# The five engines' hand-written orders replaced by another set, with some seventy small operations on other engines

## Chip, core and metric

One core of a Trainium2 chip runs the whole program. The metric is the device time of one execution in microseconds (us), and the lower the better. The engines' names are those of the profile: PE multiplies matrices (PEld is its weight load), DVE is the vector engine, ACT the engine for exponentials and scaled copies, POOL a slower vector engine, SP the engine whose queue issues nearly all transfers (DMAs).

## What is computed

Attention that is masked by clusters feeds a two-layer block with a softmax gate and a layer norm. Cut to what matters:

```python
# q, k, v: 4 batches x 8 heads x 768 positions x 64; centroids: 8 heads x 16 x 64
q_assign = argmax(q_n @ c_n.T)            # the nearest of 16 centroids, for each position
k_assign = argmax(k_n @ c_n.T)
scores = where(q_assign == k_assign, q @ k.T / 8, -1e9)
attn = softmax(scores) @ v
x = attn, heads side by side              # 3072 tokens x 512
h = x @ w_in                              # 3072 x 1024
solu = h * softmax(h)
ln = (solu - mean) / sqrt(var + 1e-6) * g_ln
out = ln @ w_out                          # 3072 x 512
```

## The kernel before, in words

**Tiles and stages.** There are 16 pairs of heads (4 batches, 4 pairs each). For each pair, q and k are loaded and turned so that the head dimension lies on partitions (by PE for the first batch, operations `tp`, L396 and L403; by DVE for the others, `xt`, L444), PE scores them against the centroids (`cl`, L484 and L489), DVE finds the best centroid of each position (`tb`, `mx`, `oh`, `ot`), and 32 rows with the one-hot assignment are placed below the cast q and k (`ca`, L468 to L472; `pl`, L533 to L540; `bl`, L549), so that one matmul gives score and mask together.

The scores are worked off in 94 units of a few (head, 128-query block) pieces. A unit's scores lie in banks of PSUM, each 128 keys by 512 queries (by 384 in the first four units). `S24.0` is the scores of bank 0 of unit 24: PE writes them (function `scores`, L627; two matmuls of 256 columns, or one of 384 in the first four units). `E24.0` is the exponential of that bank on ACT (function `expo`, L635), and `V24.0` and `V24.1` are the products with v on PE (function `values`, L654, six matmuls of 65 columns each). `N` is the division on DVE (L666, L679). There are 294 banks. After a token tile of 128 has all its heads, `tx` turns x, `h` (96 operations of two matmuls of 512 columns, L744) and `y` (96 such, L813) are the two layers, and `hm`, `ex`, `u`, `tu`, `bn`, `ag`, `at`, `al`, `sc`, `ou` are the maximum, the exponential, the product, its turning, the norm's statistics, the scale and the store.

**What sets the order.** Every operation is entered with `add`: a name, an engine, a cost, what it needs, and a function that issues its instructions. The class `Weave` holds a text for each engine with the kinds in the order in which that engine runs them (`S2` means two operations of kind S, the next two that are not yet taken); within one engine nothing overtakes. The tables `AWAY` put single operations on another engine than their default. `run` walks through the five queues with the costs, gives each operation a start, and then issues all operations in the order of these starts, so the instruction order of each engine is the text's. The costs and the constants (`HOP`, `LANES`, `ring_s = 3`, `ring_e = 9`) are used for that walk alone; on the chip the instructions wait on semaphores that the tile framework sets from the tiles that they touch.

**Banks for scores.** The pool `ps_s` (L214) has three buffers of one bank, all with the tag `sps`. Score banks take them in turn (L622). Of the 25th to 66th bank, two in every five go to the region `hreg` instead (L614 to L616). A further tile of the same tag is made ahead of everything else: `idle_p` (L854). It takes the output of the filler matmuls: `idle(n)` (L856 to L859) issues n matmuls of 128 columns on a zeroed tile, with no reader. The operation `wm` is 25 of them at the start; each `fl` in PE's text is two more, and the text says where (L902 to L904). A tile of a pool holds its buffer until the last instruction in the program that touches it; the framework lets the next tile of that tag have the buffer from then on. In the kernel before, PE's text has `fl9`, the last filler, two operations ahead of `S0.0`.

**The start.** The first pair comes in halves. `tp0.0.x.y` turns half y of q (x = 0) or k (x = 1) of the first pair; `tp0.1.0.0` to `tp0.3.1.1` are the other pairs of batch 0, twelve operations of three matmuls. Their data come by two transfers of 384 KB for each pair (`load_twelve`, L377).

**The end.** The last tile but one (f = 22) and the last (f = 23) are turned by PE (`ptu`), copied to SBUF by `tu` (L738 on DVE, L740 on ACT), multiplied (`y`) and scaled by `sc` (L830 on ACT, L832 on DVE).

Of the kernel before, what the change touches and what calls it, by code (L numbers as in the profile page):

```python
# [22 lines left out]
class Weave:  # L23
# [18 lines left out]
    ORDER["PE"] = """
        fl wm tp2 cp fl4 cl tp2 fl4 cl fl tp S2 cq S tp S tp S2 tp S tp2 S2 cl S V3 S2 tp3 S gt V3
        S2 tp2 S tp S2 cl S3 V3 S7 V3 S3 cl S3 V4 S5 V2 S V2 S4 V S2 V3 S cl S3 V2 S V S2 V S me S3
        V S V3 me S3 ptx V2 S2 cl V S V S5 V2 h4 S2 h V2 S3 h V2 S V2 S h S2 h S V S V2 S V S h S2 h
        V S2 V2 S y3 V S2 y S h2 S2 V2 h2 S2 cl S V S V2 S V S h S2 h S V S V S h y4 S3 V3 h2 S2 V2
        S h S2 V y S y3 S2 V2 S cl S V S V S V2 S2 y S y S2 V3 S2 y S V S y S2 V2 S h S2 V3 S2 cl S
        V3 S3 cl S2 V2 S V2 S h2 S3 h V S V S V2 y3 S2 y V S2 V h S2 V S h S V S h2 S3 h V2 S2 V4 h
        S3 y3 S2 V y S2 V3 S2 h2 S3 V2 cl S3 V2 h S2 h cl V2 S2 V2 S h S2 h2 S2 V3 y S y S y S y V S
        V2 S h2 S2 h2 S3 V3 S V y3 V y V S2 h S cl S3 V2 h S2 h V S2 V S cl V2 S3 y2 S V S V y2 h2  # L50
        S2 V2 S h2 S3 cl S V3 S V S2 y3 S2 V y V S h S2 h V2 S h2 S3 h V2 S y2 S V2 S2 V2 y2 S2 h3
        S3 V2 h2 V y S3 y3 V3 S3 h2 S2 cl S V S V S V2 S y2 h V S2 h V S2 h2 S2 V S V h V4 S2 y2 h
        S3 V2 h2 S2 V2 S y2 S2 h2 y2 S h2 S2 V2 y S V2 S y h2 S3 h2 S2 V4 y S3 h2 y V S2 h2 V S V S
# [5 lines left out]
        bn hm tb N mx oh bn ag ot u xt2 hm cv N bn u bn2 tb mx hm bn N oh ag2 u ot xt2 hm bn N sc u
        bn tb ag cv N xt mx oh xt ot sc N bl xt2 tb bn N mx ca tb N mx oh ot hm oh N ot u xt bn3 ag  # L60
        xt N ag hm sc N ca u bn2 xt bl sc hm ag N xt tb mx u tb oh ot N hm mx xt oh u bn2 ot N hm bn
        ag xt ca u N bn tb xt2 mx ag hm tb N bn2 oh ot u xt2 N hm tb mx oh N ag bn bl u mx bn ot N
        bn oh hm ot ag xt u N bn xt ag hm bn2 ag u sc N bl hm ca tb mx cv2 oh u ot N bn2 hm N bl u
# [8 lines left out]
    """
    AWAY = {}
    AWAY.update(dict.fromkeys("""
        ca0.0.0.0.0 ca0.0.0.1.0 ca0.0.0.1.1 ca0.2.0.0 ca0.2.1.0 ca3.2.0.1 sc23.0 xa0.0.0.1 xa0.0.1.0
        xa0.1.1.1 xa0.2.0.0 xa0.2.0.1 xa0.2.1.0 xa0.2.1.1 xa0.3.0.0 xa0.3.1.0 xb0.0.1.1
    """.split(), "ACT"))
    AWAY.update(dict.fromkeys("""
        bl0.0.1 bl1.3 bl2.1 bl3.0 bl3.1 bl3.3 ca0.1.0.0 ca0.1.0.1 ca0.2.1.1 ca2.1.0.0 ca2.2.1.0
        ca3.0.0.1 ca3.3.1.0 cv0.0.0 cv0.1.0 cv1.1.0 cv1.2.0 cv3.1.1 cv3.2.1 cv3.3.0 pl0.0.0.0.1  # L80
        pl0.0.0.1.1 sc11 sc13 sc14 sc18 sc2 sc23.1 sc3 sc4 sc5 tu22.0
    """.split(), "DVE"))
    AWAY.update(dict.fromkeys("""
        ca0.0.1.1.1 pl0.0.0.0.0 pl0.0.0.1.0 pl0.0.1.0.0 pl0.0.1.1.0 pl1.0.0.0 pl1.0.0.1 pl1.0.1.0
        pl1.0.1.1 pl1.1.0.0 pl1.1.0.1 pl1.1.1.0 pl1.1.1.1 pl1.2.0.0 pl1.2.0.1 pl1.2.1.0 pl1.2.1.1
        pl1.3.0.0 pl1.3.0.1 pl1.3.1.0 pl1.3.1.1 pl2.0.0.0 pl2.0.0.1 pl2.0.1.0 pl2.0.1.1 pl2.1.0.0
        pl2.1.0.1 pl2.1.1.0 pl2.2.0.0 pl2.2.0.1 pl2.2.1.0 pl2.2.1.1 pl2.3.0.0 pl2.3.0.1 pl2.3.1.0
        pl2.3.1.1 pl3.0.0.0 pl3.0.0.1 pl3.0.1.0 pl3.1.0.0 pl3.1.0.1 pl3.1.1.0 pl3.1.1.1 pl3.2.0.0
        pl3.2.0.1 pl3.2.1.0 pl3.2.1.1 pl3.3.0.0
    """.split(), "POOL"))  # L90
    HOP = 0.17
    LANES = 8
# [1232 lines left out]
```

## Time and profile before

| what | value |
|---|---|
| time, median of 3 runs (lowest to highest) | 224.29 us (224.18 to 224.49) |
| span of the profiled execution | 222.4 us |
| granted PE clock in the profiled execution | 0.999 |
| DVE busy | 199.1 us (90%) |
| POOL busy | 126.6 us (57%) |
| DMA mean | 174 GB/s |

The profiled execution is one run of the same program, from its first to its last instruction; the median lies 1.9 us above its span, which is what lies around the span. An engine's busy time is the union of its instructions. Matmuls overlap in the records (the end of one is modelled), so PE's pace is read from the distance between starts, or from the chain of waits, where each piece stands with the time until the next. 30 matmuls of L744 and L813 have no record; those of L627 are complete, so a score bank is found by counting its matmuls.

### The profile page before, as it was taken

What the parts mean: (1) busy time and instruction counts of PE and PEld (TensorE: products, weight loads), DVE (VectorE), ACT (ScalarE), POOL (GpSimd) and SP (SyncE); (2) the same over time, 40 slices, a digit from 0 to 9 for tenths busy, and PEclk for the clock granted to TensorE, in tenths of its full rate; (3) what the DMA queues carried; (4) which work ended last, traced back from release to release, by engine and by line L of the source; (5) the groups of instructions that cost most, each with busy time, mean ns of one, the idle gap of its engine ahead of it and who ended that gap; (6) DMA issues with size and microseconds to landing.
All of it is one profiled execution on the core that took longest, in us unless ns stands there. A gap on an engine that the chain in (4) does not pass through costs nothing.

```text
span 222.4 us, 6852 instructions
## 1 busy us (share of the span) xinstructions
PE 214.8 (97%) x2518; PEld 151.8 (68%) x2548; DVE 199.1 (90%) x363; ACT 194.7 (88%) x382; POOL 126.6 (57%) x252
## 2 busy tenths in 40 slices
PE   8999899999999999999999999999999999999993
PEld 7765577767777687777777666676767767665452
DVE  2789999999999999899989999999999979999891
ACT  3899999999999999999999989999999989795352
POOL 3189597759884986188837674783746101226131
PEclk9999999999999999999999999999999999999999
DMA  6998989797799979899999897998922928565623
GB/s 157 352 388 221 193 165 284 203 172 165 127 175 237 180 141 215 136 193 166 153 211 239 156 185 150 151 168 158 230 99 50 115 78 145 117 165 121 166 98 143
DMA packets 122433, 38.74 MB, mean 174 GB/s; under 512 B 111448, under 2 KB 117152, under 8 KB 122400
## 3 DMA queue, kind: packets, MB, share of 16 engines
q1 hardware_dynamic: 121680, 37.82, 79.8%
q10 hardware_dynamic: 720, 0.49, 0.7%
q8 instruction: 20, 0.33, 0.7%
q14 instruction: 13, 0.11, 0.1%
HBM read 23.11 MB, written 6.29 MB: 132 GB/s over the span
## 4 chain that ended last, share of the span: by engine, by line
PE 91%; DVE 3%; issue 2%; ACT 2%; DVEq 0%; ACTq 0%
PE sps L627 27%; PE hreg L744 18%; PE yps L813 17%; PE ops L654 16%; PE csc L489 4%; PE hreg L627 2%; PE idle_p L859 2%; PE csc L484 1%; PE hreg L403 1%; PE hreg L396 1%; ACT qk L468 1%; PE hreg L813 1%; ACT e L635 1%; DVE u L763 1%; DVE w_sum L598 1%
## 5 line engine op out<-in xcount | busy, mean ns | idle before, releaser
L635 ACT ACTIVATE e<-sps 128x512 bf16<-128x512 f32 (+1 forms) x276 | 143.2, 609 | 10.2 <-PE sps L627 9.8
L627 PE MATMUL sps<-qk 96*128 96x256 bf16 (+5 forms) x600 | 87.4, 263 | 0.7 <-ACT e L635 0.4
L627 PEld LDWEIGHTS <-qk 96*128 96x128 bf16 (+1 forms) x636 | 59.6, 121 | 24.5 <-issue 8.8
L654 PEld LDWEIGHTS <-e 128*128 128x128 bf16 x1152 | 49.9, 97 | 9.3 <-issue 1.9
L654 PE MATMUL ops<-v,e 128*128 128x65 bf16 x1152 | 54.3, 193 | 0.4 <-DVE x L679 0.4
L744 PE MATMUL hreg<-w_in_sb,xT 128*128 128x512 bf16 x177 | 48.3, 378 | 0.8
L813 PE MATMUL yps<-w_out_c,uT 128*128 128x512 bf16 x169 | 45.1, 379 | 0.8
L540 POOL COPY qk<-oht 32x384 f32<-32x384 f32 (+1 forms) x49 | 24.2, 494 | 21.5 <-DVE oht L521 15.7
L763 DVE TENSOR_TENSOR u<-e_sb,hreg 128x1024 bf16<-128x1024 bf16 (+1 forms) x25 | 29.1, 1169 | 2.7 <-ACT e_sb L756 2.1
L774 DVE BATCH_NORM_STATS2 bs<-u 128x6 f32<-128x512 bf16 x48 | 31.3, 677 | 0.0
L750 DVE TENSOR_REDUCE nmax<-hreg 128x1 f32<-128x1024 f32 x24 | 29.1, 1213 | 2.0 <-PE hreg L744 1.7
L756 ACT ACTIVATE e_sb<-hreg,nmax 128x1024 bf16<-128x1024 f32 x24 | 26.9, 1121 | 4.5 <-DVE nmax L750 4.4
L790 POOL TENSOR_SCALAR esq<-es,mv 128x1 f32<-128x1 f32 x24 | 8.3, 344 | 33.6 <-DVE mv L778 30.3
L813 PEld LDWEIGHTS <-uT 128*128 128x128 bf16 x200 | 18.0, 97 | 13.1 <-issue 0.3
L744 PEld LDWEIGHTS <-xT 128*128 128x128 bf16 x192 | 17.6, 97 | 11.3 <-ACT e L635 0.3
L472 POOL TENSOR_SCALAR qk<-xt 64x768 bf16<-64x768 f32 (+1 forms) x27 | 22.2, 823 | 3.5 <-DVE xt L444 1.7
L444 DVE STREAM_TRANSPOSE xt<-raw 128x768 f32<-128x768 f32 x24 | 22.2, 949 | 0.0
L470 POOL CAST qk<-xt 64x768 bf16<-64x768 f32 (+1 forms) x25 | 20.9, 836 | 1.2
L679 DVE TENSOR_TENSOR x<-ops,den 128x256 bf16<-128x256 f32 (+1 forms) x39 | 18.9, 486 | 1.3
L784 POOL TENSOR_SCALAR es<-esum 128x1 f32<-128x1 f32 x24 | 5.6, 236 | 20.9 <-ACT e_sb L756 20.4
L793 POOL TENSOR_TENSOR alpha<-esq,halves 128x1 f32<-128x1 f32 x24 | 13.8, 574 | 2.0
L830 ACT ACTIVATE y<-yps,alpha 128x512 f32<-128x512 f32 x15 | 10.4, 695 | 4.3 <-PE yps L813 3.0
(85 smaller groups left out, 206.9 us busy)
## 6 DMA issues: line engine op xcount, KB each, us to landing
vf<-in_v_dram SPq DMA_DIRECT2D x16, 384.0 KB, 4.6
out_dram<-y SPq DMA_DIRECT2D x23, 256.0 KB, 2.5
raw<-in_q_dram SPq DMA_DIRECT2D x50, 96.0 KB, 3.8
raw<-in_k_dram SPq DMA_DIRECT2D x50, 96.0 KB, 3.0
w_g<-in_moe_w_out_dram SPq DMA_DIRECT2D x4, 512.0 KB, 8.3
w_st<-in_moe_w_in_dram SPq DMA_DIRECT2D x4, 512.0 KB, 6.2
raw<-in_q_dram SPq DMA_DIRECT2D x3, 384.0 KB, 6.0
raw<-in_k_dram SPq DMA_DIRECT2D x3, 384.0 KB, 7.8
```

The lines of the kernel that those rows point to most:

```text
L444: nc.vector.transpose(xt[:], raws[b, p, i][:].rearrange("p j c -> p (j c)"))
L472: VEC[e].tensor_scalar(dst, src, scalar1=inv_C, scalar2=1.0, op0=Alu.mult, op1=Alu.mult)
L540: ins = VEC[e].tensor_copy(dst.bitcast(F32), src.bitcast(F32).unsqueeze(1) .to_broadcast([NB, 2, n // 2]))
L627: ins = nc.tensor.matmul(sps_[n, k][:, c0:c0 + w], side(b, h // 2, 1, h % 2, keys)[r], side(b, h // 2, 0, h % 2, slice(s0 * P, s0 * P + w) ...
L635: ins = nc.scalar.activation(es[n, k][:, :w], sps_[n, k][:, :w], Act.Exp, scale=exp_scale, bias=-exp_scale)
L654: nc.tensor.matmul(opss[g][:, s, :VW], es[n, k][:, c0:c0 + P], v1[slot(b, h // 2)][:, h % 2, kt, :VW], start=(kt == 0), stop=(kt == n_t - 1))
L744: uses(nc.tensor.matmul(hreg[:, at(f, f2)[1], :], xTs[f][:, dc, :], w_in_sb[:, dc, f2 * FF2:(f2 + 1) * FF2], start=(dc == 0), stop=(dc == ...
L750: uses(nc.vector.tensor_reduce(ff[f, "nmax"][:], pair_of(f), axis=AXY, op=Alu.max, negate=True), *both(f))
L756: uses(nc.scalar.activation(ff[f, "e"][:], pair_of(f), Act.Exp, bias=ff[f, "nmax"][:], accum_out=ff[f, "esum"][:]), *both(f))
L763: uses(nc.vector.tensor_tensor(ff[f, "u"][:, r], ff[f, "e"][:, r], pair_of(f)[:, r], op=Alu.mult), *both(f)[r])
L774: nc.vector.bn_stats(ff[f, "bs"][:, f2, :], ff[f, "u"][:, f2, :])
L813: ins = nc.tensor.matmul(dst, ff[f, "uT"][:, at(f, f2)[0] * (n_fc // 2) + c, :], w_out_c[:, fc, cols], start=(fc == fcs[0] and turn == 0 i ...
```

## The change

Only the texts and the tables at the head of `Weave` differ: the order of all five engines, and the engine of 74 operations. No operation is added or taken away: PE has 733 before and after, with ten `fl` in both. Between engines there move: 12 of the `pl` from POOL to SP and 3 from SP to POOL, 3 from POOL to DVE, 1 from DVE to POOL; casts `ca`: 7 from DVE to POOL, 4 from POOL to DVE, 4 from POOL to ACT, 4 from ACT to POOL, 2 from ACT to DVE; `cv`: 6 from DVE to POOL, 5 back; `bl`: 5 from DVE to POOL, 3 back; copies `xa`: 3 from DVE to ACT, 3 from ACT to DVE; scales `sc`: 3 from DVE to ACT, 4 from ACT to DVE; both copies `tu22` from DVE to ACT.

The diff, cut:

```diff
     ORDER["SP"] = """
-        ld4 si ld3 lv lg ld3 lo lv lo ld2 lo2 lv ld6 lv ld8 li4 tx ld3 lv ld tx lv tu ld10 tx tu ld4
...
+        ld4 si ld4 lg lv ld lo lv ld5 lo ld5 lv ld2 lo ld lo ld lv ld li ld2 li3 ld3 tx ld2 tx lv ld
+        lv ld tu ld2 tx ld3 pl2 tu ld lv ld5 tu ld7 pl ou tu ld lv ld4 ou ld4 pl ld2 tu ld lv ld4 ou
...
     ORDER["PE"] = """
-        fl wm tp2 cp fl4 cl tp2 fl4 cl fl tp S2 cq S tp S tp S2 tp S tp2 S2 cl S V3 S2 tp3 S gt V3
-        S2 tp2 S tp S2 cl S3 V3 S7 V3 S3 cl S3 V4 S5 V2 S V2 S4 V S2 V3 S cl S3 V2 S V S2 V S me S3
-        V S V3 me S3 ptx V2 S2 cl V S V S5 V2 h4 S2 h V2 S3 h V2 S V2 S h S2 h S V S V2 S V S h S2 h
-        V S2 V2 S y3 V S2 y S h2 S2 V2 h2 S2 cl S V S V2 S V S h S2 h S V S V S h y4 S3 V3 h2 S2 V2
...
-        V y4 S2 V h4 S3 y V3 y S2 y2 h4 y S V3 y V y2 h ptx h y h2 y3 h2 y4 h2 ptu2 y8 ptu y4 ptu y4
+        fl wm fl tp2 cp tp cl tp3 cl tp2 S2 cq S tp S2 tp S tp S2 cl S3 tp V3 S tp gt S tp S V3 S cl
+        S3 tp S tp S V S V2 S fl S2 fl S4 V S V2 S2 cl S V S2 V S V2 S3 fl S3 V2 S V2 S fl S cl S V
+        S V3 S4 V S2 V2 S V S3 fl me S2 V4 me S3 V S2 ptx V S V S V S2 cl S V S V2 h S V S h S2 V S
+        h S h V S V S V S2 h S fl V h fl V2 S2 V h S2 h S2 h S V S V2 S2 V h S V y2 V S y2 S h2 S2 h
+        cl S h V2 S V S V S2 V2 h S2 h S h S V y V S V2 S y2 V y h S V S2 y S y S2 h S2 y2 V h V2 S2
+        V S cl S V S V S2 y S y V2 S2 V2 y S h V S V S y S2 h S2 h S V3 S cl S2 V h S2 V2 S2 cl S V
+        S V2 S V fl S2 y S V S y V S V2 y S3 V y h2 S2 V S V2 h S2 h S2 V h S2 h V2 S2 V2 S y3 V S y
...
+        S2 h3 S V2 y V2 y3 h ptx h y h2 y3 h2 y4 h2 ptu2 y8 ptu y3 ptu y5
     """
     ORDER["DVE"] = """
...
-        ag bn N ag2 u tx bn hm sc u bn2 hm tu2 bn ag2 u2 bn2 ag tu sc
...
+        u bn ag bn hm bn ag bn u ag N bn hm N u tx bn hm sc ag u bn2 hm bn2 ag2 u2 bn sc bn tu ag
+        sc3
     """
     ORDER["ACT"] = """
-        wa xa2 ca2 xa2 xb ca4 E6 xa E2 xa E xa ca E3 xa3 E4 ca E2 xa E53 ex E13 ex E5 sc E3 ex E11
...
-        tu sc2 oz
+        wa xa3 ca xa xb xa ca xa2 E8 xa E xa2 E3 ca E xa E64 ex E11 ex E5 sc E2 ex E8 ca E3 ex sc E8
+        sc ca E8 ex E25 ex E12 ex E5 sc E4 ex E13 ex E6 sc E3 ex E8 ca E10 ex E7 sc E6 ex E6 sc E4
...
+        sc ex sc tu3 oz
     """
```

Written out, the first part of PE's order is: before, `fl0 wm tp0.0.0.0 tp0.0.1.0 cp fl1 fl2 fl3 fl4 cl0.0.0 tp0.0.0.1 tp0.0.1.1 fl5 fl6 fl7 fl8 cl0.0.1 fl9 tp0.1.0.0 S0.0`; after, `fl0 wm fl1 tp0.0.0.0 tp0.0.1.0 cp tp0.0.0.1 cl0.0.0 tp0.0.1.1 tp0.1.0.0 tp0.1.0.1 cl0.0.1 tp0.1.1.0 tp0.1.1.1 S0.0`. The eight other fillers stand, after the change, behind `S3.3`, `S3.5`, `S8.1`, `S10.0`, `S14.1`, `S22.1`, `h1.0.1` and, as the last one, `fl9`, behind `S43.0 V41.1`.

More of the change, by code (lines that the diff above doesn't have):

```diff
@@ L34 @@
+        lv ld tx ou ld3 tu ld tx pl ld10 tx ld tu lv ld2 tu ou ld lv ld ou ld5 lv ld4 pl ld2 tu2 ou
+        ld ou ld lv ld pl ld3 ou tx tu pl lv tx tu ou ld2 pl2 tu ou tu ou pl2 tx lv pl2 ou tu tx tu
+        ou tu tx2 ou tx tu ou tu2 tx ou tu ou2 tu ou5
     """
     ORDER["POOL"] = """
-        pl2 bl pl3 ca pl ca cv ca3 pl3 bl ca pl ca pl cv z2 pl3 ca bl z cv2 ca pl4 sg bl cv2 wi ca
-        wi7 ca3 at pl4 z cv ca2 cv bl cv al pl2 ca3 at pl2 z bl ca3 al at al pl4 at ca cv ca cv ca
-        cv al bl ca3 pl4 ca2 pl4 at2 pl2 bl ca cv pl al2 ca2 cv2 ca2 at cv ca4 al pl4 at2 cv bl cv3
@@ L39 @@
-        pl2 al pl2 ca2 bl ca at al ca pl2 cv2 pl ca3 al ca3 pl at2 pl3 al2 ca2 pl ca at cv pl cv at
-        ca at cv al pl2 bl pl al at3 al2 at al2 at al at al2 at2 po at al3
+        ca3 pl2 z bl pl z pl ca pl ca pl ca z ca cv pl2 cv ca bl ca2 pl2 ca pl z ca pl ca cv2 ca pl
+        sg pl bl pl2 cv2 ca wi2 pl3 ca z wi3 pl wi bl wi2 ca cv ca at cv ca al ca pl at pl ca2 at cv
+        ca al pl2 ca bl al ca cv pl ca at ca pl2 al pl at ca cv ca bl ca pl4 cv ca cv2 ca at ca al
+        ca2 pl2 ca3 cv bl ca al pl3 ca pl cv at al cv pl bl ca at2 cv al ca pl2 al bl pl ca pl at ca
@@ new lines @@
+        S V2 S V fl S2 y S V S y V S V2 y S3 V y h2 S2 V S V2 h S2 h S2 V h S2 h V2 S2 V2 S y3 V S y
+        S2 h2 S2 cl S V2 S3 cl V3 S V S h2 S2 h V S V S h V S3 V y V S V y S y S h S y V S h S V h
+        S2 h V4 S2 y S2 y V S h y V y S V S2 V S h S cl V S2 V S h S cl h S V2 S V S2 V3 S2 y3 h S2
+        V2 S2 y V S2 V h S h S3 h cl S V2 S2 V y V y S y S V S V h V S2 h S V S y h2 S V S y S2 y V
+        h S2 y V2 h y S2 V2 h2 S h V S V y S y2 V S y S V h3 S2 V2 S cl h S3 h V2 y S V S V S2 h V
@@ L59 @@
[L59 to L63, printed above, removed]
@@ L64 @@
-        cv ag bn2 hm N bn u sc hm N u bn2 hm N bn ag u bn sc hm ag N bn u bn2 hm bn N ag2 u bn2 hm
-        ag bn N ag2 u tx bn hm sc u bn2 hm tu2 bn ag2 u2 bn2 ag tu sc
+        cn xb cb ca2 tb mx oh ot pl2 tb mx oh ot xa cf ca xa bl cv ca cv tb mx oh ot gk pl su xa pl
+        N su tb xa2 mx oh ot xt su N xt tb su N bl mx oh ot N su2 tb N mx su oh su N xt ot N ce xt
+        tx ce N ce4 N ce2 tb hm N xt u bn2 N cv mx hm ag oh ot u cv bn xt hm N bn u bn ag N tb hm bl
+        mx oh bn ot xt ag u xt N xt2 hm bn tb mx N oh ot xt bn ag u N bn sc xt2 tb cv mx oh N bn ot
@@ new lines @@
+        tb ag N hm mx bl N oh ot u bn xt N sc hm bn ag xt u xt N bn hm tb mx bn u N tb bn oh mx ag
+        ot hm xt N oh u xt ot bn hm ag N bn xt bn sc ag xt u cv tb xt N xt tb hm N mx oh ot bn u bn
+        ca N ag mx bn oh tb hm N xt ot bn u N hm ag mx bn ca u oh ot N hm xt bn ag u bn2 ag hm bn N
+        tb bn u mx oh N hm bn ot u ag bn2 hm N ag bn ag u bn N sc hm bn N u bn hm N u sc hm bn ag N
+        u bn ag bn hm bn ag bn u ag N bn hm N u tx bn hm sc ag u bn2 hm bn2 ag2 u2 bn sc bn tu ag
@@ L72 @@
+        ex E4 ca sc E2 ex E2 sc E5 ex E12 ex E2 sc E5 ex E8 ex E7 ex E5 ex sc E6 ex E4 sc E ex sc ex
+        sc ex sc tu3 oz
     """
@@ L74 @@
     AWAY.update(dict.fromkeys("""
-        ca0.0.0.0.0 ca0.0.0.1.0 ca0.0.0.1.1 ca0.2.0.0 ca0.2.1.0 ca3.2.0.1 sc23.0 xa0.0.0.1 xa0.0.1.0
-        xa0.1.1.1 xa0.2.0.0 xa0.2.0.1 xa0.2.1.0 xa0.2.1.1 xa0.3.0.0 xa0.3.1.0 xb0.0.1.1
+        ca0.0.0.0.0 ca0.2.0.0 ca1.2.1.1 ca2.0.0.0 ca3.0.0.0 ca3.2.1.0 tu22.1 xa0.0.0.1 xa0.0.1.0
+        xa0.1.0.0 xa0.1.0.1 xa0.1.1.0 xa0.2.0.0 xa0.2.0.1 xa0.2.1.1 xa0.3.0.0 xb0.0.1.1
     """.split(), "ACT"))
     AWAY.update(dict.fromkeys("""
-        bl0.0.1 bl1.3 bl2.1 bl3.0 bl3.1 bl3.3 ca0.1.0.0 ca0.1.0.1 ca0.2.1.1 ca2.1.0.0 ca2.2.1.0
-        ca3.0.0.1 ca3.3.1.0 cv0.0.0 cv0.1.0 cv1.1.0 cv1.2.0 cv3.1.1 cv3.2.1 cv3.3.0 pl0.0.0.0.1
-        pl0.0.0.1.1 sc11 sc13 sc14 sc18 sc2 sc23.1 sc3 sc4 sc5 tu22.0
+        bl0.0.1 bl0.2 bl1.1 bl2.0 ca0.0.0.1.0 ca0.0.1.1.0 ca0.0.1.1.1 ca0.1.1.1 ca3.0.1.0 ca3.2.0.0
+        cv0.0.0 cv0.0.1 cv1.0.0 cv1.0.1 cv1.3.0 cv2.3.1 pl0.0.0.1.1 pl0.1.0.1 pl0.1.1.1 sc13 sc14
+        sc18 sc21 sc22 sc23.1 sc3 sc4 sc7
     """.split(), "DVE"))
     AWAY.update(dict.fromkeys("""
[L84 to L89, printed above, removed]
+        ca0.0.1.0.1 pl0.0.0.0.0 pl0.0.1.0.0 pl0.0.1.1.0 pl1.0.0.0 pl1.0.0.1 pl1.0.1.0 pl1.0.1.1
+        pl1.1.0.1 pl1.1.1.1 pl1.2.0.1 pl1.2.1.0 pl1.2.1.1 pl1.3.0.0 pl1.3.0.1 pl1.3.1.0 pl2.0.0.0
+        pl2.0.0.1 pl2.0.1.0 pl2.0.1.1 pl2.1.0.0 pl2.1.0.1 pl2.1.1.1 pl2.2.0.0 pl2.2.0.1 pl2.2.1.0
+        pl2.2.1.1 pl2.3.0.1 pl2.3.1.0 pl2.3.1.1 pl3.0.0.0 pl3.0.0.1 pl3.0.1.1 pl3.1.0.0 pl3.1.0.1
+        pl3.1.1.1 pl3.3.0.0 pl3.3.1.1
     """.split(), "POOL"))
```

18 lines of the change are left out of this document (4 added, 14 removed).

## The prediction

> **What bounds the kernel now.** I read the page first, then busy time by stage, then single stretches of the timeline.
>
> ```profile
> span 222.4 us, 6852 instructions
> ...
> PE 214.8 (97%) x2518; PEld 151.8 (68%) x2548; DVE 199.1 (90%) x363; ACT 194.7 (88%) x382; POOL 126.6 (57%) x252
> ...
> PE 91%; DVE 3%; issue 2%; ACT 2%; DVEq 0%; ACTq 0%
> ```
>
> PE is busy 97% of the span, and 91% of the chain that ended last is PE work. The change adds and removes no PE work, so its best case is small: it can only fill what PE waits. I cut the span where the 1st, 25th, 67th and 142nd score bank begin (`S0.0`, `S4.0`, `S18.0`, `S43.0`), found by counting L627's matmuls, and call the stages A, B, C and the rest.
>
> ```profile
> 9.90:23.73 13.83, 13.28 (x146) 8.60 (x145) 12.52 (x26) 13.43 (x33) 11.03 (x18) 1.00 0.96 318
> 23.73:44.09 20.36, 19.79 (x287) 14.80 (x288) 19.44 (x40) 20.24 (x43) 15.47 (x29) 1.00 0.89 203
> 44.09:90.99 46.90, 46.12 (x563) 33.95 (x568) 44.22 (x76) 45.16 (x89) 33.55 (x60) 1.00 0.94 173
> 90.99:222.40 131.41, 126.74 (x1371) 87.10 (x1390) 118.40 (x204) 110.68 (x209) 63.70 (x127) 1.00 0.74 151
> ```
>
> The columns after the length are PE, PEld, DVE, ACT, POOL, the granted clock, the DMA share and GB/s. In B, ACT is busy 20.24 of 20.36 us. In C both PE and ACT are nearly full. They are coupled by the score banks, and there I look next.
>
> ```profile
> 9.31 0.28 PE L859 MATMUL idle_p<-w_out_c 128*128 128x128 bf16 x2
> 9.90 0.48 PE L627 MATMUL sps<-qk 80*128 80x384 bf16 x2
> 10.34 0.33 PE L627 MATMUL sps<-qk 80*128 80x384 bf16 x1
> 10.61 0.84 ACT L635 ACTIVATE e<-sps 128x384 bf16<-128x384 f32 x2
> 11.13 0.32 PE L627 MATMUL sps<-qk 96*128 96x384 bf16 x1
> ```
>
> The last filler runs at 9.31. Then three score banks are filled (two at 9.90, one at 10.34) before the first exponential begins at 10.61; the fourth waits for it. So three banks go round, and the tile of the fillers, which had one of the three, has given it up. How tight three are is seen here:
>
> ```profile
> 46.86 0.60 PE L627 MATMUL sps<-qk 96*128 96x256 bf16 x4
> 47.34 1.09 ACT L635 ACTIVATE e<-sps 128x512 bf16<-128x512 f32 x2 [0.40 <-PE sps L627]
> 48.39 1.11 ACT L756 ACTIVATE e_sb<-hreg,nmax 128x1024 bf16<-128x1024 f32 x1
> 49.50 4.00 ACT L635 ACTIVATE e<-sps 128x512 bf16<-128x512 f32 x8
> 50.13 0.38 PE L627 MATMUL sps<-qk 80*128 80x256 bf16 x2 [0.40 <-ACT e L635]
> ...
> L635 ACT ACTIVATE e<-sps 128x512 bf16<-128x512 f32 x252 | 133.2, 620 | 9.8 <-PE sps L627 9.4
> ```
>
> A bank's scores begin at 46.86 and its exponential, for which ACT was waiting, at 47.34: 0.48 us. An exponential takes 0.62 and back to back begins every (4.00 - 0.62) / 7 = 0.48. The one from 49.50 ends at 50.12, and the scores that need its bank begin at 50.13. So a bank that is used again at once comes round in 0.48 + 0.62 + 0.01 = 1.11 us. This was PE's one long wait in C: the softmax's exponential (1.11 us at 48.39) stood ahead of a score exponential, and three banks didn't cover it.
>
> **The change, part by part.** *The fillers* are the part that I weigh most. In PE's new text `fl9` stands behind `S43.0`, at the 142nd bank of 294. The filler tile keeps its buffer until its last use, so from `S0.0` to `S43.0` the scores have two banks of `ps_s` in place of three (in B two of every five go to `hreg` besides). 124 score banks pass through that narrower ring. It adds a wait to each: scores k wait for exponential k-2 of the ring, and behind them in PE's queue stand `V`, `h` and `y`, for which DVE and ACT wait.
>
> To price it I write PE's work between score starts along the new text, with these paces:
>
> ```profile
> 12.69 0.66 PE hreg L403 x6
> 13.68 1.43 PE csc L484 x16
> 98.00 0.44 PE sps L627 x4
> 101.90 0.38 PE ops L654 x12
> 108.40 0.86 PE hreg L744 x4
> 110.30 0.78 PE csc L489 x8
> 176.63 0.86 PE yps L813 x4
> 8.10 0.62 PE L859 MATMUL idle_p<-w_out_c 128*128 128x128 bf16 x8
> 5.72 1.06 PE L859 MATMUL idle_p<-w_out_c 128*128 128x128 bf16 x8
> ```
>
> An S is two matmuls, 0.22 (0.16 in A, one of 384 columns); V six, 0.19; h and y two, 0.43; `cl` 0.78 (1.43 for the other pairs of batch 0); a `tp` three, 0.33; an `fl` at most 0.11 (eight matmuls take 0.62 with the last one's latency). Two ring banks on, PE may not begin before 1.11 us have passed. Example: `S24.0 S24.1 h2.0.0 S24.2` has 0.22 + 0.22 + 0.43 = 0.87 us from the first to the third S, 0.24 short. Then `V22.0 S25.0 V22.1 V23.0 S25.1`: from `S24.2` to `S25.1` two S and three V, 1.01, short by 0.10. With three banks no such stretch is short by more than 0.15, before or after.
>
> C: the work before was 75 S, 52 V, 37 h or y and 4 `cl`, 45.5 us (measured 46.90, with the wait at 50.13). After: 75 S, 51 V, 40 h or y, 5 `cl`, two fillers, 47.6, so +2.1, which is taken from the rest of the kernel (-1.0) and from A and B. Of 37 disjoint pairs of steps 18 are short, 20 if I start one bank later; the largest sum over stretches that don't overlap is 5.5 us, from 22. Where ACT has an `ex`, `sc` or `ca` between two exponentials, the bank comes back later by its length. Counting these (five `ex` at 1.11, three `sc`, two `ca`) the sum is 7.6. I take 7.6, since 50.13 shows that kind of wait with three banks already; that old wait of 0.4 goes into it. C: +2.1 + 7.6 - 0.4 = +9.3, bounds +7.2 (pairs alone) and +11.
>
> B: ACT sets the pace, 20.36 / 42 banks = 0.485. Once in five banks the same bank is wanted two steps on, where 1.11 replaces 2 x 0.48: 8 x 0.14 = +1.1. By PE (work 18.1, pairs short by 2.7) it would be 20.8, +0.4. I take +1.1, bounds +0.4 and +1.5.
>
> A: PE's work falls from 12.5 to 11.7, since three `tp` go ahead of `S0.0` (-1.0) and two fillers come in (+0.2). Measured were 13.8, so 1.3 of waits. With a ring of two, and 0.95 for 384 columns (1.11 less 0.05 on PE and 0.11 on ACT), the short stretches sum to 2.8, or 3.7 with ACT's copies between: 14.5 to 15.4, and up to 16.7 if the old waits stay. I take 15.1: +1.3, bounds +0.7 and +2.9.
>
> *The start.* PE's fillers there give way to `tp0.1.0.0` to `tp0.1.1.1`, all ahead of `S0.0`, and two of these ahead of `cl0.0.1`.
>
> ```profile
> 3.33 0.43 SPq L377 DMA_DIRECT2D raw<-in_q_dram  x1
> 3.80 0.43 SPq L377 DMA_DIRECT2D raw<-in_k_dram  x1
> ...
> raw<-in_q_dram SPq DMA_DIRECT2D x3, 384.0 KB, 6.0
> raw<-in_k_dram SPq DMA_DIRECT2D x3, 384.0 KB, 7.8
> ```
>
> These data are issued at 3.33 and 3.80 and take 6.0 and 7.8 in the median. `tp0.1.0.0` ran at 9.43 before, right after the 9.31 filler. So PE stands at a load with `cl` and the first scores behind it; `S0.0` at 9.9 becomes 10.2 with the four turns done. +0.3, bounds -0.3 (the casts now spread over three engines help) and +0.6.
>
> *The engines' swaps.* Between DVE, ACT and POOL operations of the same kinds go both ways in nearly equal numbers. What is left is POOL's gain, an engine that is 57% busy:
>
> ```profile
> L540 POOL COPY qk<-oht 32x384 f32<-32x384 f32 (+1 forms) x49 | 24.2, 494 | 21.5 <-DVE oht L521 15.7
> ...
> qk<-oht SPq DMA_DIRECT2D x5, 48.0 KB, 2.0
> ```
>
> Twelve `pl` leave POOL (12 x 0.49 = 6 us), three come, and SP gets nine more DMAs that land 2.0 us after issue. A `pl` on SP waits there for DVE's `ot`, and loads and turns stand behind it; their data are used ten and more us later, so I cost it at nothing, or up to 0.4 where a `tu` behind it makes a `y` late.
>
> *The end.* `sc22` and `sc23.0` go to DVE, `tu22` to ACT.
>
> ```profile
> 218.79 0.53 ACT L830 ACTIVATE w_in_sb<-hreg,alpha 128x320 f32<-128x320 f32 x1 [0.87 <-PE hreg L813]
> 219.13 0.42 DVE L832 TENSOR_SCALAR w_in_sb<-hreg,alpha 128x192 f32<-128x192 f32 x1 [1.40 <-PE hreg L813]
> ```
>
> The last two scales ran side by side. Now DVE does both: from 218.79, 0.46 us (between 0.42 and ACT's 0.53) before the second begins, at 219.25 in place of 219.13: +0.1, bounds 0 and +0.6 (if `sc21` and `sc22` ahead of them are late).
>
> Sum: 0.3 + 1.3 + 1.1 + 9.3 - 1.0 + 0.1 = +11.1 on a span of 222.4, so 233.5. The median of the runs, 224.29, is 1.9 above the span before: 235.4 us.
>
> **Rivals.** *Three banks all along* (faster). If the filler tile's bank goes to the scores although it is used again later, no ring wait is added. Then A loses its 0.8 of work and the old 1.3 of waits, C gains 2.1 of work and loses the 0.4: 0.3 - 2.1 + 2.1 - 0.4 - 1.0 + 0.1 = -1.0, 223.3 us; with the old waits kept, 225.0. For it: PE's text after the change spreads S singly, which suits three banks (no stretch short). Against: the trace shows the bank given over only after the last filler. It decides at the third bank, `S0.2`: it begins before the first exponential ends, or after.
>
> *The clock falls in C.* The fillers show two speeds: eight in 1.06 us at 5.72, and in 0.62 at 8.10. PE so began at about half speed, for some 6 us, and one fall as long would cost 3 us: 238.4. Against it: the clock stayed at 1.00 in all stages through the 0.40 wait, and the new waits are a few tenths each, with one to two us at an `ex`. [...]
>
> **How the numbers follow.** Two banks, as summed: 0.82. The clock besides: 0.06. Three banks: 0.12, of which 0.07 faster, 0.03 too close to tell and 0.02 slower, if the old waits stay. About 0.2% is what a measurement of this kernel can tell. So faster 0.07, same 0.03, slower 0.90. The forecast's own lower end is -0.3 + 0.7 + 0.4 + 7.2 - 1.0 = +7.0, 231.3, and 2 us less if the 1.11 is 0.06 too long for some 36 stretches; the upper is 0.6 + 2.9 + 1.5 + 11 - 1.0 + 0.6 = +15.6, 239.9. The range is 229 to 241; it takes in the fall of the clock and leaves out the three banks.
>
> **What would show it.** Right: the third score bank begins after the first exponential ends; PE waits for ACT's L635 dozens of times until about 100 us and hardly after the last L859; ACT's waits for L627 rise too; the 142nd bank begins 9 to 14 us later than 90.99, and from there to the end it takes 1 us less than before; PE's busy share drops to 93%. Wrong: three banks filled before the first exponential, or a stage C under 50 us. If the last filler's place matters for nothing, the sum is wrong by its largest terms.

## The result, and the profile after

The changed kernel takes 243.31 us (median, 242.95 to 243.85) beside 224.24 for the one before on the same chip: a ratio of 1.0856, 95% interval 1.0834 to 1.0878. It is slower, as forecast, but by 19 us and not by 11, and outside the range of 229 to 241.

The page of the kernel after: the span, the busy times, and the chain of work that ended last.

```profile
span 241.5 us, 6881 instructions
...
PE 223.1 (92%) x2548; PEld 153.0 (63%) x2548; DVE 204.0 (84%) x360; ACT 200.6 (83%) x381; POOL 124.1 (51%) x247
...
PE 59%; ACT 14%; DMA 8%; DVE 7%; issue 5%; POOL 2%; SPq 2%; DVEq 0%; ACTq 0%; POOLq 0%
```

PE's share of the chain fell from 91% to 59%; ACT, DMA and DVE took its place. All three big engines have a smaller busy share than before. So no engine became the bound: they wait for each other.

By stage (columns as in the prediction), after:

```profile
10.69:25.91 15.22, 13.22 (x142) 8.22 (x140) 14.49 (x28) 12.98 (x29) 10.98 (x18) 1.00 0.89 222
25.91:49.88 23.97, 19.54 (x287) 15.19 (x285) 20.21 (x37) 21.38 (x43) 17.64 (x30) 1.00 0.85 215
49.88:107.19 57.31, 52.87 (x582) 35.47 (x580) 47.56 (x82) 50.30 (x93) 26.90 (x50) 1.00 0.80 155
107.19:241.50 134.31, 128.76 (x1393) 86.90 (x1389) 116.15 (x193) 110.83 (x209) 63.82 (x127) 1.00 0.70 143
```

The first boundary of the prediction was read 0.36 us too early: it was interpolated inside a run of scores, and the 25th bank's own first matmul stands at 24.09, not at 23.73. With that the first two stages before are these:

```profile
9.90:24.09 14.19, 13.28 (x146) 8.62 (x146) 12.88 (x27) 13.79 (x34) 11.03 (x18) 1.00 0.97 316
24.09:44.08 19.99, 19.78 (x287) 14.77 (x287) 19.07 (x39) 19.87 (x42) 15.46 (x29) 1.00 0.88 203
```

| | before | after | change | forecast |
|---|---|---|---|---|
| first score bank | 9.90 | 10.69 | +0.8 | +0.3 |
| A | 14.19 | 15.22 | +1.0 | +1.3 |
| B | 19.99 | 23.97 | +4.0 | +1.1 |
| C | 46.91 | 57.31 | +10.4 | +9.3 |
| rest with the end | 131.4 | 134.3 | +2.9 | -0.9 |

The timeline of the kernel after, at the third score bank and at the last filler:

```profile
10.69 0.49 PE L631 MATMUL sps<-qk 80*128 80x384 bf16 x2
...
11.06 1.39 ACT L639 ACTIVATE e<-sps 128x384 bf16<-128x384 f32 x3
11.60 0.32 PE L631 MATMUL sps<-qk 80*128 80x384 bf16 x1 [0.30 <-ACT e L639]
...
107.60 0.27 PE L863 MATMUL idle_p<-w_out_c 128*128 128x128 bf16 x2
```

(The kernel after has four lines more at its head, so L627 is now L631, L635 is L639, and so on.) Two banks are filled at 10.69. The third waits until 11.60, and what it waits for is the first exponential. Before, the third began at 10.34, ahead of the first exponential at 10.61. The last filler is at 107.60, and the waits of the two engines over the whole span are these (us in total, times, longest):

```profile
PE sps L631 <- ACT e L639: 8.9, 18, 0.9
```
```profile
ACT e L639 <- PE sps L631: 13.5, 31, 1.0
```

Before, these rows were the following:

```profile
PE sps L627 <- ACT e L635: 0.4, 1, 0.4
```
```profile
ACT e L635 <- PE sps L627: 9.8, 29, 1.4
```

None of PE's 18 waits lies behind the last filler. ACT waits hardly more often than before, but for longer in sum.

### The profile page after: what moved, and what is told of

The parts are those of the page before. It is cut to its first block, busy times and chain, and to the rows that moved or that the text cites. A ratio compares the mean times of both kernels' runs of the same rounds, so it can differ in the third digit from the quotient of the medians.

```text
span 241.5 us, 6881 instructions
## 1 busy us (share of the span) xinstructions
PE 223.1 (92%) x2548; PEld 153.0 (63%) x2548; DVE 204.0 (84%) x360; ACT 200.6 (83%) x381; POOL 124.1 (51%) x247
## 4 chain that ended last, share of the span: by engine, by line
PE 59%; ACT 14%; DMA 8%; DVE 7%; issue 5%; POOL 2%; SPq 2%; DVEq 0%; ACTq 0%; POOLq 0%
PE sps L631 17%; ACT e L639 12%; PE yps L817 12%; PE hreg L748 12%; PE ops L658 9%; DMA xT<-x 4%; DMA raw<-in_q_dram 3%; PE csc L493 3%; PE csc L488 2%; DMA raw<-in_k_dram 2%; PE hreg L631 2%; SPq L440 2%; DVE u L767 1%; DVE nmax L754 1%; PE hreg L407 1%
## 5 line engine op out<-in xcount | busy, mean ns | idle before, releaser
L639 ACT ACTIVATE e<-sps 128x512 bf16<-128x512 f32 (+1 forms) x276 | 147.0, 592 | 16.9 <-PE sps L631 13.5
L631 PE MATMUL sps<-qk 96*128 96x256 bf16 (+5 forms) x600 | 95.5, 263 | 10.9 <-ACT e L639 8.9
L631 PEld LDWEIGHTS <-qk 96*128 96x128 bf16 (+1 forms) x636 | 60.9, 121 | 37.5 <-issue 18.9
L658 PEld LDWEIGHTS <-e 128*128 128x128 bf16 x1152 | 53.6, 97 | 12.5 <-issue 1.3
L658 PE MATMUL ops<-v,e 128*128 128x65 bf16 x1152 | 58.8, 194 | 0.1
L748 PE MATMUL hreg<-w_in_sb,xT 128*128 128x512 bf16 x192 | 54.2, 379 | 0.7 <-DMA xT<-x 0.7
L817 PE MATMUL yps<-w_out_c,uT 128*128 128x512 bf16 x184 | 50.2, 379 | 0.5 <-DVE cst L501 0.5
L544 POOL COPY qk<-oht 32x384 f32<-32x384 f32 (+1 forms) x40 | 19.4, 484 | 42.0 <-DVE oht L525 40.3
L474 POOL CAST qk<-xt 64x768 bf16<-64x768 f32 (+1 forms) x28 | 23.0, 821 | 5.4 <-ACT xt L426 3.8
L562 POOL CAST v<-vf 128x384 bf16<-128x384 f32 x26 | 13.9, 543 | 7.7 <-DMA vf<-in_v_dram 6.3
```

The lines of the kernel that those rows point to most:

```text
L474: VEC[e].tensor_copy(dst, src)
L631: ins = nc.tensor.matmul(sps_[n, k][:, c0:c0 + w], side(b, h // 2, 1, h % 2, keys)[r], side(b, h // 2, 0, h % 2, slice(s0 * P, s0 * P + w) ...
L639: ins = nc.scalar.activation(es[n, k][:, :w], sps_[n, k][:, :w], Act.Exp, scale=exp_scale, bias=-exp_scale)
L658: nc.tensor.matmul(opss[g][:, s, :VW], es[n, k][:, c0:c0 + P], v1[slot(b, h // 2)][:, h % 2, kt, :VW], start=(kt == 0), stop=(kt == n_t - 1))
L748: uses(nc.tensor.matmul(hreg[:, at(f, f2)[1], :], xTs[f][:, dc, :], w_in_sb[:, dc, f2 * FF2:(f2 + 1) * FF2], start=(dc == 0), stop=(dc == ...
L817: ins = nc.tensor.matmul(dst, ff[f, "uT"][:, at(f, f2)[0] * (n_fc // 2) + c, :], w_out_c[:, fc, cols], start=(fc == fcs[0] and turn == 0 i ...
```

## Experiments

Theory: the filler tile keeps one of three score banks until 107 us, and this makes most of the loss. Rival: the new orders themselves make it. This table has the stages of all runs, found by counting the score matmuls of each profile (us; the time is the median of all executions, the stages are those of the one profiled; "after dropped" is after with its late fillers dropped):

| kernel | time | first bank | A | B | C | rest |
|---|---|---|---|---|---|---|
| before | 224.2 | 9.90 | 14.19 | 19.99 | 46.91 | 131.4 |
| after | 243.3 | 10.69 | 15.22 | 23.97 | 57.31 | 134.3 |
| after, late fillers early | 233.8 | 10.65 | 13.95 | 20.43 | 51.20 | 135.2 |
| after, late fillers dropped | 230.3 | 10.07 | 13.43 | 20.43 | 50.38 | 133.5 |
| before, last filler at `S43.0` | 243.6 | 9.38 | 15.93 | 27.38 | 56.84 | 131.5 |
| after, last filler at `S3.5` | 233.9 | 10.73 | 15.22 | 20.37 | 50.60 | 135.0 |
| after dropped, `pl` back on POOL | 230.6 | 10.22 | 13.21 | 20.44 | 49.66 | 134.5 |
| after dropped, then before | 228.9 | 10.08 | 13.97 | 20.44 | 50.75 | 132.1 |
| before, then after | 228.3 | 8.90 | 14.06 | 19.99 | 46.91 | 135.9 |
| after, third region in B | 239.5 | 10.20 | 15.22 | 21.18 | 57.31 | 133.7 |
| after, a tile for each late filler | 235.4 | 10.32 | 13.31 | 21.75 | 51.26 | 137.1 |
| after dropped, three operations later | 231.0 | 10.38 | 13.66 | 20.43 | 52.76 | 133.4 |
| before, no `fl1` to `fl9` | 223.9 | 9.52 | 14.21 | 19.98 | 46.92 | 131.4 |
| before, last filler at the end | 264.8 | 9.08 | 15.97 | 27.19 | 56.85 | 154.2 |

Four of these profiles hold one stretch of 3.4 us at half clock, worth up to 1.7 us (last section): both kernels with the last filler of before moved (in B), the one with a tile for each late filler (in the rest) and the one with three operations later (in C).

**One filler moved in the kernel before.**

```diff
-        fl wm tp2 cp fl4 cl tp2 fl4 cl fl tp S2 cq S
+        fl wm tp2 cp fl4 cl tp2 fl4 cl tp S2 cq S
...
-        V3 S3 cl S2 V2 S V2 S h2 S3 h V S V
+        V3 S3 cl S2 V2 S V2 S fl h2 S3 h V S V
```

> The kernel before with only its last filler moved, to behind the 142nd score bank (S43.0): two matmuls of 128 columns change place, every other order as before. Theory: the ring of two comes with it; by the stretches of the order before about +2.5 us in the first stage, +3.5 in the second, +8 in the third: 235 to 242 us, 142nd bank at 102 to 108 us. Rival (the place of the last filler matters for nothing, the orders of the other engines make the loss): 224.3 us, within 0.5.

243.64 us, ratio 1.0894 (1.0849 to 1.0939). Two matmuls that nothing reads, moved in PE's order, cost as much as the whole change. That the two sums meet is chance: under the orders of after the held tile costs 10 to 12 us, as the next runs show. The stages with the ring of two, of this kernel:

```profile
25.31:52.68 27.37, 21.74 (x287) 15.79 (x286) 22.67 (x37) 21.51 (x42) 19.27 (x33) 0.94 0.63 148
52.68:109.52 56.84, 51.09 (x570) 34.83 (x568) 45.11 (x76) 48.52 (x90) 30.16 (x55) 1.00 0.76 145
109.52:241.00 131.48, 128.09 (x1396) 87.19 (x1392) 118.75 (x204) 110.56 (x208) 63.24 (x127) 1.00 0.73 148
```

The loss stops dead behind the filler: the rest is 131.5, as before. A is 1.7 us longer, B 7.4 and C 9.9, where 2.5, 3.5 and 8 were expected, and the time lies 1.6 above the bound of 242. Most of the miss is in B; its clock is 0.94, of which more below. The rival by which the last filler's place matters for nothing falls.

**The ring of two to the end.** The same edit with the filler behind `S93.2`:

```diff
-        h4 y S V3 y V y2 h ptx
+        h4 y S fl V3 y V y2 h ptx
```

> The kernel before with its last filler behind the last score bank (S93.2), so that the ring has two banks for all 294. Theory (the loss goes with the number of banks that pass while the filler tile is held): the stages up to the 142nd bank as in the run with the filler behind S43.0 (15.9, 27.4, 56.8 us), and the last one longer by 152 banks at 0.07 to 0.13 us each, 10 to 20 us: 254 to 264 us. Rival (the loss is made once, early, and taken back where PE has room): 244 to 248 us.

264.75 us, ratio 1.1802 (1.1765 to 1.184). The stages up to `S43.0` are as in the run above within 0.2 us; the rest is 154.2 in place of 131.5, so 22.7 us for 152 banks, 0.15 each, a little over the bound that I gave. PE's waits for exponentials in this kernel:

```profile
PE sps L627 <- ACT e L635: 24.6, 43, 1.3
```

The loss goes with the number of banks that pass while the tile is held. Nothing is taken back later.

**The same orders, another tile.** Here all orders are those of the kernel after; each late filler takes a bank of its own.

```diff
+    def idle(n, own=False):
+        to = ps_s.tile([P, FF2], F32, name="idle_q", tag="sps") if own else idle_p
...
-        add(f"fl{j}", "PE", 0.11, 0, lambda e: idle(2))
+        add(f"fl{j}", "PE", 0.11, 0, lambda e, j=j: idle(2, j > 1))
```

> The kernel after with every order as it is and the eight late fillers at their late places; only, each of these writes to a bank that it takes from the ring for itself, in place of the tile made at the start, which is last used by fl1. Theory (the tile that is kept makes the loss, not the fillers' places): ring waits nearly gone, third score bank at 11.1 us and ahead of the first exponential's end, 142nd bank at 94 to 97 us, 230 to 234.5 us. Rival (fillers among the scores are what costs): 238 us or more.

235.43 us: 7.9 less than after, though above my bound of 234.5. The timeline at the third bank:

```profile
10.32 0.49 PE L631 MATMUL sps<-qk 80*128 80x384 bf16 x2
...
10.69 1.64 ACT L639 ACTIVATE e<-sps 128x384 bf16<-128x384 f32 x4
10.76 0.33 PE L631 MATMUL sps<-qk 80*128 80x384 bf16 x1
```

The third bank no longer waits. A, B and C are 1.9, 2.2 and 6.0 us shorter than after, 10.2 in all. That is the least that the held tile costs under these very orders, since each late filler still takes one bank out of its turn (PE waited 1.0 us for one such bank). The rest is 2.8 longer than after: a fall of the clock (below) is part of it, and PE waited there 3.1 us for the turned x, against 0.7 in after.

**The late fillers early, or dropped.**

```diff
-        fl wm fl tp2 cp tp cl tp3 cl tp2 S2 cq S
+        fl wm fl tp2 cp fl8 tp cl tp3 cl tp2 S2 cq S
```

(and the eight `fl` among the scores go; the second run has them in neither place, so it leaves out matmuls that nothing reads).

> The kernel after, with its eight late fillers moved ahead of the first score bank (behind the turn of the centroids, cp); all else as after. Theory (the late last filler keeps one of the three score banks until 107 us, and that makes most of the 19 us): the third score bank begins before the first exponential ends, no wait for L639 of the ring kind in the second and third stage, 142nd bank at 91 to 95 us, time 225 to 230 us. Rival (the new orders of SP, POOL, DVE and ACT make the loss): 240 us or more, as after (243.3).

> The kernel after without its eight late fillers: these matmuls, which nothing reads, are left out. Theory: as the run with early fillers within 1 us, 225 to 230 us, since the fillers' own work (8 x 0.11 = 0.9 us) stood where PE waited for loads. Rival (the fillers' work among the scores costs, not the bank): this run gains what the early fillers do not; then it is at least 2 us under that run.

233.79 us (ratio 1.0441, 1.0395 to 1.0487) and 230.34 (1.0289, 1.0255 to 1.0323). Three banks take away 9.5 to 13 us. But both stay above before, though their ring has three banks all along, and above my bounds. So the rival holds for a part: without the held tile the new orders still cost 6 to 7 us, or 10 with the fillers at the start. Where that is, in the run with the fillers dropped:

```profile
10.07:23.50 13.43, 12.42 (x139) 7.75 (x137) 12.89 (x27) 11.95 (x30) 10.86 (x18) 1.00 0.94 242
23.50:43.93 20.43, 18.59 (x279) 14.47 (x279) 19.59 (x38) 19.32 (x40) 17.63 (x30) 1.00 1.00 253
43.93:94.31 50.38, 49.89 (x578) 34.74 (x576) 47.69 (x82) 48.13 (x94) 27.32 (x50) 1.00 0.94 168
94.31:227.80 133.49, 128.13 (x1393) 86.84 (x1389) 116.40 (x195) 110.67 (x210) 64.25 (x128) 1.00 0.70 149
```

A is 0.8 shorter than before, B 0.4 longer, C 3.5 longer, the rest 2.1. PE's waits of this kernel name what came in:

```profile
PE sps L631 <- POOL qk L537: 1.8, 2, 1.2
...
PE hreg L748 <- DMA xT<-x: 0.9, 2, 0.5
...
PE csc L493 <- ACT y L834: 0.5, 1, 0.5
```

The first is in B: POOL is busy there for 15.0 of the 16 us from 28 to 44, with casts between its `pl`. It doesn't appear in the kernel after, perhaps since the ring's waits let POOL catch up, so that one wait hid another. It costs little, since B is 0.4 longer only. That the two runs differ by 3.5 us isn't explained by 0.9 us of fillers. It is the sign that I had set for the rival of the second run (fillers among the scores are what costs), though neither run has fillers there; it can't account for the 7.9 us above, where the fillers stayed in their late places. Of the 3.5, 0.6 lie before the first bank and 1.7 in the rest, where the run with early fillers has this row in place of the 0.9:

```profile
PE hreg L748 <- DMA xT<-x: 2.4, 3, 1.5
```

Why the turned x comes later there stays open.

**The ring of two in the first stage alone.** As the run with early fillers, but two are left in place, the last behind `S3.5`:

```diff
-        fl wm fl tp2 cp tp cl tp3 cl tp2 S2 cq S
+        fl wm fl tp2 cp fl6 tp cl tp3 cl tp2 S2 cq S
...
         S3 tp S tp S V S V2 S fl S2 fl S4 V S V2
...
-        S2 cl S V S2 V S V2 S3 fl S3 V2
+        S2 cl S V S2 V S V2 S6 V2
```

> The kernel after with six of its late fillers moved ahead of the first score bank and two left in place, the last one behind the 24th score bank (S3.5): a ring of two through the first stage (24 banks) alone. Theory: 1.3 to 2.6 us above the run with all of them early, nearly all of it before the 25th bank begins; the second and third stage as in that run. Rival (a late filler costs the same wherever it is): as after, 243 us.

A is 15.22, to the hundredth that of after, and 1.3 above the run with all of them early, the lower end of what was expected. The time is the same (233.85 and 233.79) and not 1.3 to 2.6 longer: C and the rest gave 0.9 us back. So of a stall of one stage not everything need reach the end.

**More banks in B.** The kernel after, with five more of B's banks in `hreg`.

```diff
-    slots = {BANKS[i]: (i - spare_from) % 5 for i in range(spare_from, spare_to)
-             if (i - spare_from) % 5 < 2}
+    slots = {BANKS[i]: (0, 1, 9, 9, 2)[(i - spare_from) % 5] for i in range(spare_from, spare_to)
+             if (i - spare_from) % 5 < 2 or (i - spare_from) % 5 == 4 and i < 52}
```

> The kernel after, fillers and all, but in the second stage five more score banks (the 29th, 34th, 39th, 44th and 49th, the last of each five) go to the third bank of hreg, so that of every five banks three stand outside the ring. Theory (too few banks ahead make the second stage 24.0 us long instead of 20.4): it falls to 20.4 to 22 us, the first and third stages stay within 0.5 us, 240 to 241.7 us in all. Rival (the new order of DVE and POOL, oh, ot and pl, makes that stage long): it stays within 0.5 us of 24.0, 243.3 us in all.

239.46 us, a little under the 240 to 241.7 expected. The first three stages of this kernel:

```profile
10.20:25.41 15.21, 13.21 (x142) 8.22 (x140) 14.48 (x28) 12.94 (x29) 10.73 (x19) 1.00 0.94 236
25.41:46.59 21.18, 19.08 (x287) 15.05 (x285) 19.02 (x37) 20.54 (x43) 18.21 (x31) 1.00 0.99 241
46.59:103.91 57.32, 52.86 (x583) 35.48 (x581) 47.55 (x82) 50.31 (x93) 26.73 (x49) 1.00 0.79 153
```

B falls from 23.97 to 21.18, and A and C stay to 0.01 us. PE's waits for exponentials in B were 4.7 us in 8 of the kernel after; here they are:

```profile
PE sps L631 <- ACT e L639: 1.8, 3, 0.9
PE hreg L631 <- ACT e L639: 0.3, 1, 0.3
```

So the greater part of B's loss is too few banks ahead, and not the order of DVE and POOL.

**What the orders cost by themselves.** Four runs without a tile that is held through the stage in question. In the first the twelve `pl` go back; of SP's and POOL's texts the first places that change:

```diff
-        lv ld tu ld2 tx ld3 pl2 tu ld lv ld5
+        lv ld tu ld2 tx ld3 tu ld lv ld5
...
-        cv ca al ca pl at pl ca2 at cv
+        cv ca al pl ca pl2 at pl ca2 at cv
```

> The kernel after without its eight late fillers (nothing reads their output), and with the twelve pl that went from POOL to SP given back to POOL, each ahead of the operation that would start next there; all else as after. It stands beside the run with the fillers dropped (230.3 us). Theory (a pl in SP's queue holds back the turn of x behind it, and PE's first h of a tile waits for it): PE's waits for the turned x (0.71 and 0.51 us) go, 228.8 to 229.6 us. Rival (the places of loads and turns in SP's new order do it, whoever runs the pl): 230.3 us, within 0.4.

230.58 us: nothing gained, as the rival had it. The twelve `pl` on SP, which the prediction had costed at nothing, cost nothing that can be told. (C is 0.7 shorter and the rest 1.0 longer, where PE waits once 1.6 us for a scale on ACT.)

The next two are cut at `S43.0`: each engine runs what stands ahead of the cut in the one kernel, and from there what is left, in the order and on the engines of the other. ACT's text of the first beside that of the kernel after, from the cut on:

```diff
-        E8 ex E25 ex E12 ex E5 sc E4 ex E13 ex E6 sc E3 ex
+        E8 ex E24 ex E15 ex E15 ex E9 ex E3 sc E8 ex sc E14 ex
```

> The kernel after without its eight late fillers up to the 142nd score bank (S43.0), on every engine; from there the orders and engines of the kernel before. Theory (the last stage's loss is made by the new order of that stage): that stage takes 130.5 to 131.8 us in place of 133.5, so 227.2 to 228.6 us in all. Rival (it is inherited: SP and POOL come late into the last stage): 133 us or more there, 229.8 to 230.8 in all.

> The reverse: the kernel before, its ten fillers too, up to the 142nd score bank; from there the orders and engines of the kernel after. Theory (the new order of the last stage has waits of its own, some 2 us): the 142nd bank begins at 91.0 as before, and the last stage takes 133 to 134 us: 225.9 to 226.9 us. Rival (nothing is wrong with that order by itself): 224.3 us, within 0.5.

228.87 and 228.28 us, 0.3 and 1.4 above the bounds. In the first the rest falls from 133.5 to 132.1, short of what the theory wanted by 0.3. In the second the rest rises from before's 131.4 to 135.9, more than forecast, with the stages ahead of it as before. So the new order of the last stage loses time by itself; some of the 4.5 us may be the seam between the two orders, where things stand otherwise than either expects. The chain of waits of the second, from 90 to 222 us:

```profile
by line: PE hreg L744 22.6%; PE sps L627 22.0%; PE yps L813 21.4%; PE ops L654 12.4%; DMA xT<-x 10.4%; PE csc L489 3.1%; issue 1.5%; PE hreg L813 1.1%; ACT e L635 0.9%; DVE u L763 0.9%; DVE xt L444 0.7%; PE utp L732 0.7%; DVE bs L774 0.6%; 
```

The transfer that turns x has 10.4% of the chain. In the kernel before it has no share in this stretch. PE's listed waits in the rest say the same. Before has none there. After and the six runs with its orders throughout (the one whose clock fell there left out) have 1.1 to 2.9 us, mostly for the turned x and for ACT's scales. Without these waits their rest is 132.1 to 132.8 us, whether it was 133.4 or 135.2, and that of before then after is 133.3. So half or more of this stage's loss is such waits, and nearly all of the scatter between these runs; 0.7 to 1.4 us of it (1.9 in before then after) have no listed wait. One such turn, in the run with the fillers dropped (timelines of DVE, SP and PE):

```profile
95.15 0.42 DVE L683 TENSOR_TENSOR x<-ops,den 128x256 bf16<-128x256 f32 x1
...
95.94 1.61 SPq L713 DMA_TRANSPOSE xT<-x  x1
...
99.92 1.04 PE L748 MATMUL hreg<-w_in_sb,xT 128*128 128x512 bf16 x4 [0.54 <-DMA xT<-x]
```

From x written (95.57) to the first `h` that may use it are 4.3 us; the order gives it less. I then moved back the operations that wait most:

```diff
-        S3 V y h2 S2 V S V2 h
+        S3 V y S2 V h2 S V2 h
...
-        V S y S2 h2 S2 cl S V2 S3 cl V3
+        V S y S2 h2 S3 V2 cl S3 cl V3
...
-        S V S V h V S2 h S V S y
+        S V S V2 S2 h2 S V S y
```

> The kernel after without its eight late fillers (nothing reads their output), and three operations of PE moved back by about the wait that they had there: h6.0.0 and h6.0.1 (0.71 us) behind V44.1, cl2.2 (0.65) behind V49.1, h12.0.0 (0.51) behind S71.0. It stands beside the run with the fillers dropped (230.3 us). Theory (in the last stage the new order wants the turned x 0.5 to 0.7 us before the transfer has it, and that is a wait of its own): 228.3 to 229.4 us. Rival (behind PE's wait the exponentials or DVE are as late): 230.3 us, within 0.5.

231.03 us, ratio to before 1.0329 (1.0298 to 1.036): no gain. The three waits are gone, and the rest is 133.4 as it was, with PE waiting for exponentials in their place. The simple reading (a few `h` are placed too early) falls. In C, whose orders are as they were, this profile is 2.4 us longer; a wait of 0.83 us and a fall of the clock behind it stand there, and the execution profiled was the slowest of the six (232.69).

**The fillers of the kernel before.**

```diff
-        fl wm tp2 cp fl4 cl tp2 fl4 cl fl tp S2 cq S
+        fl wm tp2 cp cl tp2 cl tp S2 cq S
```

> The kernel before without fl1 to fl9 (nothing reads their output; wm and fl0 stay). Theory (they only fill time in which PE waits for loads and copies): 224.3 us, within 0.5, perhaps 0.3 less. Rival (they keep the clock up): the first score bank begins 0.5 us or more later than 9.9 us, 224.8 to 226 us.

223.9 us, ratio 0.999 (0.9976 to 1.0003): no difference that can be told. The nine fillers save nothing here that can be told, and the larger part of the change's cost hangs on operations that could have been left out. No version tried beats the kernel before by a margin that can be told.

## Why the prediction was wrong in size

*The mechanism held.* The third bank waits for the first exponential, PE's waits for L639 are many until 107 us and none later (18, where dozens were said), and PE's busy share is 92% (93% were said). Two signs missed: the 142nd bank comes 16 us later (9 to 14 were said), and from there to the end it takes 2.9 us more, not 1 less. The rival with three banks all along is out at `S0.2`. The clock rival is out too: each stage of after has 1.00.

*The held tile was priced right in sum, wrong in its parts.* With the ring alone the prediction had A +2.1 (15.1 against 13.0), B +1.1 and C +7.6, 10.8 us. After less the run with a tile for each filler gives 1.9, 2.2 and 6.0, or 10.2; after less the run with the fillers dropped gives 1.8, 3.5 and 6.9, or 12.3. In **B** the step "once in five banks the same bank is wanted two steps on" failed (+1.1, where 2.2 to 3.5 were measured): it took ACT's mean pace and let each wait end with itself. But B's PE has `cl` and `me` among the scores, and ACT had 0.12 us to spare in 20. With fewer banks ahead, such a piece can leave ACT without work; so it did here, in the chain of the kernel after and in ACT's waits in B:

```profile
37.53 0.78 PE csc L493 x8
38.31 0.33 PE hreg L631 x2
...
ACT e L639 <- PE hreg L631: 0.5, 1, 0.5
```

(The exponential of that bank began at 38.73.) ACT stood idle for 2.6 us of B, and for 0.6 of it in the run with a third region. In A and C the miss is the other way: 2.1 and 7.6 were said, at most 1.9 and 6.9 measured.

*The orders were priced wrong, and this is the larger part of the miss.* The sum had +0.3 for all but the ring (0.3 - 0.8 + 1.7 - 1.0 + 0.1); the run without held tile is 5.4 above the span before. The step that failed is the rest, "-1.0" by "taken from the rest of the kernel" (-0.9 with the end): it measured +2.9 in after and +2.1 with the ring whole. I moved PE's work between stages as if PE were never kept waiting, and asked of the new order only whether it is short of banks. What it gives to a turn of x, to a cast ahead of a `pl` or to an `al` ahead of a scale I costed at nothing, because the numbers moved each way were nearly equal. C's +3.5 with the fillers dropped holds some 1.9 of work (2.1 less two fillers); the other 1.6 have no wait over 0.2 us listed, and lie mostly behind scores: from their starts to the next start on PE, C's 150 score matmuls take 18.5 us, against 17.3 in before then after, whose C is that of before. The rival "three banks all along" went wrong by the same step: 223.3 us were forecast, and 230.3 to 235.4 were measured in three ways of making it.

*What stays open.* Which of the reordered operations makes the last stage's 2 us: giving back the `pl` did nothing, and moving the operations that wait moved the wait. Which of C's short waits come from which engine's order wasn't tried either. The price of the orders is therefore measured as a whole and only in part traced to single waits.

The start (+0.8, bounds -0.3 and +0.6) can't be read finer: in before and the run of before then after, whose orders are the same there, the first bank began at 9.90 and 8.90; in after, the run with a third region and the one with a tile for each late filler at 10.69, 10.20 and 10.32.

## What to carry to other kernels

In these runs a tile of a ring was held to its last use in the program, whatever uses it: two matmuls that nothing reads, moved behind `S43.0`, took the kernel before to 243.64 us (ratio 1.0894), and a tile for each late filler took after from 243.31 to 235.43. So before moving a step, even an idle one, look at which tile it touches and how long that tile now lives. What a narrower ring costs grows with the banks that pass through it, some 0.05 to 0.15 us each here where the clock held. A change of order had a price of its own here (6 to 7 us with the late fillers dropped), and equal numbers moved both ways didn't make it zero.
